# Local and pooled attention feeding a two-layer network: wider column chunks, and pooled rows added straight from their tile

## The chip, the cores and the metric

The kernel runs on one core of a Trainium2 chip. The metric is the device time of one execution in microseconds; a kernel's time is the median of its runs.

## What is computed

For 8 sequences, 8 heads, 576 positions and 64 features a head, two attentions are added: a dense softmax attention over queries, keys and values averaged in groups of 4 (each pooled output row serves 4 positions), and a local one, in which a position sees the 3 positions on either side. The sum, as 4608 rows of 512, goes through a network without biases.

```
out_d  = sm_attn(mean4(q), mean4(k), mean4(v))          # 144 rows a head
out_up = np.repeat(out_d, 4, axis=2)
scores = where(abs(i - j) < 4, scale * q @ k.T, -1e9)   # local, 7 keys a row
x      = out_up + softmax(scores) @ v
h      = x @ w_in                # 4608 x 512 by 512 x 2048
out    = np.maximum(0.01 * h, h) @ w_out                # back to 512
```

## The kernel before

Every matmul of the network is done in three products of a high and a low float32r part: `xh`, `xl` for the rows, `wi` pairs for `w_in`, `woh`, `wol` for `w_out`, `gh`, `gl` for the activations. The rows are the moving columns of TensorE, and they are worked off in **chunks**. `plan()` (L48) lays them out: chunk 0 has 512 columns (the first 512 positions of sequence 0, in two halves of 256), chunk 1 has 256 and chunks 2 to 11 have 384 each. The list `SIZES` gives each chunk its number of blocks: the 576 positions of a sequence are 64 groups of 9, and block j is the j-th position of all 64, 64 columns; 63 blocks belong to sequences 1 to 7.

For each of the 16 tiles f of the inner dimension, `up_proj` (L1038) makes 12 matmuls (4 contraction tiles by 3 products) into a PSUM bank `hp`, and `leaky` (L1067) turns it into `gh` (ScalarE) and `gl` (ScalarE, then VectorE). `down_proj` (L1079) makes 12 matmuls from them into `acc0` to `acc3`. There are three `gh` and three `gl` tiles, so at most three steps stand between up and down. The last two chunks, 10 and 11, are multiplied together in a Strassen scheme (`finale`, L1319), whose combinations T1 to T4 are split by `split_x24` and `split_x31`.

The rows of a chunk come from the local attention, in **segments** of up to three blocks for half the heads (u = 0 or 1): `scores` (L868) multiplies on GpSimd and sums on VectorE, `weigh` does the softmax, `values` (L937) multiplies on GpSimd again and sums on VectorE into an `xloc` tile, of which there are two. `widen` (L984) copies the pooled output `outd` on ScalarE four times along the row into one `up` tile, 576 wide, for each segment. `landing` (L1000) transposes the blocks on TensorE into a `pt` bank (L1007), adds `up` on VectorE (L1013), and splits the sum into high and low part in the chunk's x buffer (L1028, L1030). There are two x buffers, `x0` and `x1`, taken in turn, so chunk i can land once chunk i-2 has been through the up projection.

At the start the weights arrive as float64, in raw tiles (`convert`, L323), and are split: a cast on ScalarE, an integer step (L337) and a subtraction (L350) on VectorE. For f below 9 the raw tiles are the two `prod` tiles, the `up` tile and three staging tiles in `x1`. At the same time sequence 0 goes through a banded form of the local attention, whose pooled output is added at L817.

The order of all instructions is written by a planner in the program (`Order`): tasks ask for slots and engines, the planner holds a modelled clock for each engine and emits the operation that could start first, by rank among equals. So each engine's order is fixed when the program is built, and a change of sizes can move it.

Of the kernel before, what the change touches and what calls it, by code (L numbers as in the profile page):

```python
# [28 lines left out]
SIZES = (3,) + (6,) * 10  # L29
# [48 lines left out]
assert CHUNKS[LAST - 1][1] == EN and LAST % 2  # L78


def pieces(j0, j1):
    n = j1 - j0
    k = -(-n // 3)
    cuts = [j0 + n * i // k for i in range(k + 1)]
    return list(zip(cuts, cuts[1:]))


LANDED = {(i, 0): 2 * sum(len(pieces(a, z)) for _, a, z, _ in c[2]) + (i == 1) for i, c in enumerate(CHUNKS) if i}
LANDED.update({(0, a): NC for a, _ in TOP})
XMAX = [max(c[1] for c in CHUNKS[i:LAST:2]) for i in range(2)]  # L90
# [7 lines left out]
KEPT, LAND = ("x0", "x1", "gh", "gl", "o"), ("xloc", "up", "outd")  # L98
# [111 lines left out]
def attn_moe(ctx: ExitStack, tc, qkt, vm, vr, vmb, vrb, qb, kb, vb, vwb, band, identb, w_in, w_out, ident, edge, out):  # L210
# [76 lines left out]
    heads = [axp.tile([128, DM], I32, name=f"head{i}") for i in range(bufs["head"])]  # L287
# [71 lines left out]
    def outd_tile(b):  # L359
# [3 lines left out]
        t = yield from wait(("read", b), 8 if b < BANDED else 2 * len(PARTS[b]))  # L363
        s.free(t)

    def x_tile(i):
# [500 lines left out]

    def scores(b, j0, j1, u):  # L868
# [19 lines left out]
        for p in range(2):  # L888
            s_q, s_k, q, k, tl = got[p]
            for a, z in pieces(j0, j1):  # L890
                n = z - a
                s_p = yield from slot("prod")
                pr = sb(s_p, [128, 3 * W * D], F32)
                prv = pr[:, :n * W * D].rearrange("p (j t d) -> p j t d", j=n, t=W)
                tp = yield from op("POOL", n * W * D, tl, s_p.t)
                nc.gpsimd.tensor_tensor(  # L896
                    out=prv,
                    in0=q[:, a - j0:z - j0].unsqueeze(2).to_broadcast([128, n, W, D]),
                    in1=view(k, (a - j0) * D, [[D, n], [D, W], [1, D]]),
                    op=ALU.mult)  # L900
                t = yield from op("DVE", n * W * D, tp, s_s.t)
                nc.vector.tensor_reduce(out=s[:, u, p, a - j0:z - j0], in_=prv, axis=AX.X, op=ALU.add)  # L902
                s_p.free(t)
# [33 lines left out]
    def values(i, b, j0, j1, c0, u):  # L937
# [46 lines left out]
    def widen(i, b, j0, j1, u):  # L984
        to = yield from wait(("pooled", b, 2 * u))
        to = max(to, (yield from wait(("pooled", b, 2 * u + 1))))
        tx = yield from wait(("xbuf", i))
        yield from wait(("upturn", ORD[b, j0, u]))
        s_u = yield from slot("up")
        od.signal(("upturn", ORD[b, j0, u] + 1))  # L990
        up = sb(s_u, [128, 2, SD, FAC], F32)
        t = yield from op("ACT", 2 * S, s_u.t, to, times=2)
# [2 lines left out]
        od.signal(("read", b), t)
        ups[b, j0, u] = up
        od.signal(("up", b, j0, u), max(t, tx))
        s_u.free((yield from wait(("upread", b, j0, u), len(pieces(j0, j1)))))

    def landing(i, b, j0, u, a, z, col, s_x, xl_t, t):  # L1000
# [501 lines left out]
```

## Time and profile before

| | |
|---|---|
| median of 3 runs | 911.89 us (911.55 to 912.01) |
| span of the profiled execution, first to last instruction | 910.3 us |
| TensorE busy, matmuls | 897.6 us, 6129 |
| GpSimd, VectorE, ScalarE busy | 625.9, 610.1, 460.9 us |
| DMA | 119.68 MB, 131 GB/s in the mean |

The files give no other time of the profiled execution than its span; the median stands 1.6 us above it. A busy time is the sum of the instructions of an engine; matmuls overlap, so a matmul's own duration is longer than the distance to the next one. PE is TensorE, PEld its weight loads, DVE VectorE, ACT ScalarE, POOL GpSimd. L numbers are lines of the kernel before.

### The profile page before, as it was taken

The numbers are of one execution on the slowest core, as the hardware profiler recorded it, in microseconds if no ns is written. First come the engines' busy times: TensorE is split into PE (matmuls) and PEld (weight loads), VectorE is DVE, ScalarE is ACT, GpSimd is POOL, SyncE is SP. The second block draws the span as 40 slices with busy tenths as digits, with TensorE's granted clock in tenths as the row PEclk, the third lists the DMA queues.
The fourth block names the chain that finished last, engine by engine and source line by source line (L and its number), as shares of the span: only waits on it lengthen the run. The fifth ranks groups of instructions, "written<-read, shape, count | busy, mean of one in ns | idle before, by whom it ended". The sixth has DMA issues, their size and how long they took to land. (4 is left out here: it accounts for less than half of the span.)

```text
span 910.3 us, 16167 instructions
## 1 busy us (share of the span) xinstructions
PE 897.6 (99%) x6129; PEld 870.5 (96%) x6129; DVE 610.1 (67%) x887; ACT 460.9 (51%) x1277; POOL 625.9 (69%) x308
## 2 busy tenths in 40 slices
PE   8999999999999999999999999999999999999998
PEld 4789999999999999999999999999999999999998
DVE  6899889888878977875746863762863755533322
ACT  5788567666455634554324553533413425455332
POOL 4221299989989999967974964982993986787100
PEclk9999999999999999999999999999999999999999
DMA  9786566657646644652522751630431410100001
GB/s 294 257 297 240 174 205 207 199 161 216 199 124 200 210 117 121 207 176 64 153 86 76 213 161 27 176 106 27 122 113 45 122 53 1 36 1 1 1 35 36
DMA packets 61774, 119.68 MB, mean 131 GB/s; under 512 B 7248, under 2 KB 24016, under 8 KB 61696
## 3 DMA queue, kind: packets, MB, share of 16 engines
q1 hardware_dynamic: 61696, 118.65, 42.0%
q8 instruction: 48, 0.79, 0.3%
q14 instruction: 30, 0.25, 0.1%
HBM read 109.18 MB, written 9.44 MB: 130 GB/s over the span
## 5 line engine op out<-in xcount | busy, mean ns | idle before, releaser
L1060 PE MATMUL hp<-x,wi 128*128 128x384 f32 (+1 forms) x2112 | 367.4, 323 | 4.5 <-DVE gl L1074 3.6
L1060 PEld LDWEIGHTS hp<-x,wi 128*128 128x128 f32 x2112 | 338.3, 189 | 8.8 <-DVE gl L1074 4.8
L969 POOL TENSOR_TENSOR prod<-v,s 128x1344 f32<-128x1344 f32 x84 | 261.8, 3124 | 62.2 <-DVE xloc L975 57.6
L896 POOL TENSOR_TENSOR prod<-q,k 128x1344 f32<-128x1344 f32 x84 | 265.9, 3171 | 52.7 <-DVE s L902 27.0
L1098 PE MATMUL acc<-gh,woh 128*128 128x384 f32 (+1 forms) x768 | 252.3, 329 | 0.0
L1098 PE MATMUL acc<-gh,wol 128*128 128x384 f32 (+1 forms) x768 | 247.1, 322 | 0.1
L1098 PE MATMUL acc<-gl,woh 128*128 128x384 f32 (+1 forms) x768 | 246.8, 321 | 0.0
L1071 ACT ACTIVATE gh<-hp 128x384 fp32r<-128x384 f32 (+1 forms) x184 | 85.3, 464 | 223.0 <-PE acc L1098 216.8
L1074 DVE TENSOR_TENSOR gl<-hp,gh 128x384 fp32r<-128x384 f32 (+1 forms) x184 | 95.2, 518 | 133.6 <-ACT hp L1072 130.0
L1098 PEld LDWEIGHTS acc<-gh,woh 128*128 128x128 f32 x768 | 144.8, 189 | 2.5 <-issue 2.0
L1098 PEld LDWEIGHTS acc<-gh,wol 128*128 128x128 f32 x768 | 144.8, 188 | 0.5 <-DVE wol L350 0.5
L1098 PEld LDWEIGHTS acc<-gl,woh 128*128 128x128 f32 x768 | 145.0, 189 | 0.0
L902 DVE TENSOR_REDUCE s<-prod 128x21 f32<-128x1344 f32 x84 | 129.3, 1541 | 13.9 <-POOL prod L896 13.9
L975 DVE TENSOR_REDUCE xloc<-prod 128x192 f32<-128x1344 f32 x80 | 123.4, 1543 | 5.1 <-POOL prod L969 5.1
L1072 ACT ACTIVATE hp<-hp 128x384 f32<-128x384 f32 (+1 forms) x184 | 84.4, 459 | 0.0
L1013 DVE TENSOR_TENSOR pt<-pt,up 128x384 f32<-128x384 f32 x42 | 37.6, 895 | 24.6 <-PE pt L1007 22.4
L994 ACT COPY up<-outd 128x576 f32<-128x576 f32 x84 | 52.1, 672 | 0.0
L425 DVE TENSOR_REDUCE v_d<-vs 128x128 f32<-128x512 f32 (+1 forms) x56 | 37.6, 671 | 5.9 <-DMA vs<-in_vrb_dram 5.0
L1028 ACT CAST x<-pt 128x384 fp32r<-128x384 f32 x38 | 18.4, 484 | 35.7 <-DVE pt L1013 35.7
L783 POOL TENSOR_TENSOR xloc<-xloc,lst 128x280 f32<-128x280 f32 (+1 forms) x8 | 7.3, 919 | 27.0 <-ACT pd L512 12.2
L1170 POOL TENSOR_TENSOR sr<-sr 128x256 f32<-128x256 f32 x32 | 23.8, 758 | 0.9
L1170 POOL TENSOR_TENSOR sr<-wi 128x512 f32<-128x512 f32 x16 | 20.6, 1291 | 3.9 <-DVE pt L1013 3.8
(231 smaller groups left out, 1028.4 us busy)
## 6 DMA issues: line engine op xcount, KB each, us to landing
k<-in_kb_dram SPq DMA_DIRECT2D x84, 288.0 KB, 3.3
v<-in_vb_dram SPq DMA_DIRECT2D x84, 288.0 KB, 2.9
qk<-in_qkt_dram SPq DMA_DIRECT2D x32, 576.0 KB, 4.9
q<-in_qb_dram SPq DMA_DIRECT2D x84, 96.0 KB, 2.0
vs<-in_vmb_dram SPq DMA_DIRECT2D x28, 256.0 KB, 2.8
out_dram<-olot SPq DMA_DIRECT2D x36, 192.0 KB, 2.0
vs<-in_vrb_dram SPq DMA_DIRECT2D x28, 192.0 KB, 3.0
x<-in_w_in_dram SPq DMA_DIRECT2D x9, 511.8 KB, 6.2
```

What stands on the lines that cost most here:

```text
L425: nc.vector.tensor_reduce(out=v_d[:rows, k], in_=vs, axis=AX.X, op=ALU.add)
L896: nc.gpsimd.tensor_tensor(out=prv, in0=q[:, a - j0:z - j0].unsqueeze(2).to_broadcast([128, n, W, D]), in1=view(k, (a - j0) * D, [[D, n], [ ...
L902: nc.vector.tensor_reduce(out=s[:, u, p, a - j0:z - j0], in_=prv, axis=AX.X, op=ALU.add)
L969: nc.gpsimd.tensor_tensor(out=prv, in0=view(v, 0, [[1, nj], [nv, D], [1, W]]), in1=s[:, p, :nj].unsqueeze(2).to_broadcast([128, nj, D, W]) ...
L975: nc.vector.tensor_reduce(out=xl_t[:, :nj, p], in_=prv, axis=AX.X, op=ALU.add)
L994: nc.scalar.copy(out=up[:, pp], in_=outd[b][:, 2 * u + pp].unsqueeze(2).to_broadcast([128, SD, FAC]))
L1060: nc.tensor.matmul(hp[:, :n], w[h][:, ws], x[:, c], start=c + j == 0, stop=c == NC - 1 and j == 2)
L1071: nc.scalar.activation(out=gh[:, :n], in_=hp[:, :n], func=AF.Prelu, alpha=0.01)
L1072: nc.scalar.activation(out=hp[:, :n], in_=hp[:, :n], func=AF.Prelu, alpha=0.01)
L1074: nc.vector.tensor_tensor(out=gl[:, :n], in0=hp[:, :n], in1=gh[:, :n].bitcast(F32), op=ALU.subtract)
L1098: nc.tensor.matmul(acc[:, a:z], w[h][:, es], g[:, :n], start=(a, f, j) == (0, 0, 0), stop=f == NF - 1 and j == 2, skip_group_check=ch == 0)
L1170: (nc.vector if eng == "DVE" else nc.gpsimd).tensor_tensor(out=out, in0=in0, in1=in1, op=alu)
```

## The change

`SIZES` becomes (3, 6, 6, 6, 6, 8, 8, 8, 6, 6): chunk 1 keeps 256 columns, chunks 2 to 5 and 9, 10 have 384, and chunks 6 to 8 have 512. Segments of three blocks stay as they are for `scores`, `weigh` and `values`; where a chunk ends inside one, it lands in two parts, and its `xloc` tile is held until the second. `widen` and the `up` tile are gone: `landing` adds the pooled rows from `outd` in small pieces, one for each run of `RUNS`, in which the pooled row goes on by two. Steps of 256 columns share a `gh` and a `gl` tile by pairs. Both x buffers are 512 wide; the tiles `head` lie in `x1` at first and `edge` in another pool. In the Strassen pair, which is now chunks 9 and 10, T4 lies in the spare columns of one x buffer and in the other.

```diff
-SIZES = (3,) + (6,) * 10
+SIZES = (3, 6, 6, 6, 6, 8, 8, 8, 6, 6)
...
-    parts = {b: [] for b in range(BANDED, B)}
+    parts = {b: [(j, j + MAXSEG, []) for j in range(0, BLK, MAXSEG)] for b in range(BANDED, B)}
...
-            room = min(BLK - j, z - g)
-            m = -(-room // -(-room // MAXSEG))
+            _, j1, lands = parts[b + BANDED][j // MAXSEG]
+            m = min(j1 - j, z - g)
             mine.append((b + BANDED, j, j + m, c0))
-            parts[b + BANDED].append((i + 1, j, j + m, c0))
+            lands.append((i + 1, j, j + m, c0))
...
+def runs(j):
+    at = [(BLK * r + j) // FAC for r in range(FAC)]
+    cuts = [0] + [r for r in range(1, FAC) if at[r] != at[r - 1] + 2] + [FAC]
+    return [(r0, r1, at[r0]) for r0, r1 in zip(cuts, cuts[1:])]
...
-    s = yield from slot(*(("prod", "up") if f < FREE else ("stage2",) if FSPLIT < f < LSPLIT else ()), "stage")
+    s = yield from slot(*(("prod",) if f < FREE else ("stage2",) if FSPLIT < f < LSPLIT else ()), "stage")
...
-        both = sb(s_x, [128, 2, NC, XMAX[i % 2]], F32R)[:, :, :, :CHUNKS[i][1]]
+        whole = sb(s_x, [128, 2, NC, 512], F32R)
+        both = whole[:, :, :, :CHUNKS[i][1]]
+        if i == LAST - 1:
+            fin["spare"] = whole[:, :, :, EN:].rearrange("p h c n -> p (h c) n")
...
-        od.spawn(90 + 10 * b + j0 + 0.5 * u, landing(i, b, j0, u, a, z, c0, s_x, xl_t, t))
+        for k, (i, a, z, col) in enumerate(lands):
+            od.spawn(90 + 10 * b + a + 0.5 * u, landing(i, b, j0, u, a, z, col, s_x, xl_t, t, k == len(lands) - 1))
...
-    def widen(i, b, j0, j1, u):
...
-        for pp in range(2):
-            nc.scalar.copy(out=up[:, pp], in_=outd[b][:, 2 * u + pp].unsqueeze(2).to_broadcast([128, SD, FAC]))
...
-        t = yield from op("DVE", 270 * n, t, tu)
-        nc.vector.tensor_tensor(out=xv, in0=xv, in1=upv, op=ALU.add)
-        od.signal(("upread", b, j0, u), t)
+        adds = [(m, *run) for m in range(n) for run in RUNS[a + m]]
+        t = yield from op("DVE", 128 * n, t, to, times=len(adds))
+        for m, r0, r1, o in adds:
+            part = view(xps, m * 128 + r0, [[NBLK, 2], [FAC, NBLK // FAC], [1, r1 - r0]])
+            nc.vector.tensor_tensor(out=part, in0=part, in1=view(outd[b], 2 * u * SD + o, [[SD, 2], [BLK, NBLK // FAC], [2, r1 - r0]]), op=ALU.add)
...
     def leaky(i, n, s_h, hp, t):
-        s_g, s_l = (yield from slot("gh")), (yield from slot("gl"))
-        gh, gl = sb(s_g, [128, OMAX], F32R), sb(s_l, [128, OMAX], F32R)
+        half = isinstance(i, int) and n == OMAX // 2
+        if half and i % 2:
+            yield from wait(("pair", i // 2))
+            s_g, s_l, gh, gl = pairs.pop(i // 2)
+        else:
+            s_g, s_l = (yield from slot("gh")), (yield from slot("gl"))
+            gh, gl = sb(s_g, [128, OMAX], F32R), sb(s_l, [128, OMAX], F32R)
+            if half:
+                pairs[i // 2] = s_g, s_l, gh[:, n:], gl[:, n:]
...
     def split_x24():
...
+        tx = yield from wait("x1free")
+        t = yield from wait(("T", (0, 1)))
+        hi, lo, src = fin["t4"], fin["spare"][:, :6], raw[0, 1].rearrange("p c (k n) -> p (c k) n", n=512 - EN)
+        t = yield from halve(hi, lo, src, 2 * EN, "DVE", t, tx)
...
     def split_x31():
         yield from wait(("over", LAST - 2))
-        s_x = yield from slot("x1")
+        s_x = yield from slot(f"x{LAST % 2}")
...
+        od.signal("x1free", s_x.t)
```

## Rows read from the trace of the kernel before

**Rows 1.** The page: busy time of each engine, and TensorE's share by 40 slices.

```profile
PE 897.6 (99%) x6129; PEld 870.5 (96%) x6129; DVE 610.1 (67%) x887; ACT 460.9 (51%) x1277; POOL 625.9 (69%) x308
...
PE   8999999999999999999999999999999999999998
```

**Rows 2.** By stretch: length, PE, PEld, DVE, ACT, POOL busy, clock, DMA.

```profile
140.00:160.00 20.00, 19.30 (x168) 18.77 (x168) 19.07 (x27) 14.80 (x47) 19.40 (x7) 1.00 0.62 206
...
850.00:911.00 61.00, 56.61 (x327) 56.29 (x325) 17.11 (x31) 19.39 (x41) 0.00 (x0) 0.98 0.08 27
```

**Rows 3.** Waits of TensorE over the span: total us, times, longest.

```profile
PE hp L1060 <- DVE gl L1074: 3.6, 4, 1.4
...
PE hp L1060 <- DVE wi L350: 0.8, 2, 0.5
```

**Rows 4.** Timeline of TensorE, two early waits: start, us, what, idle before.

```profile
131.49 1.34 PE L1060 MATMUL hp<-x,wi 128*128 128x256 f32 x9 [1.12 <-DVE gl L1074]
...
152.51 3.14 PE L1060 MATMUL hp<-x,wi 128*128 128x256 f32 x24 [0.70 <-DVE gl L1074]
```

**Rows 5.** The chain that ended last, one piece: start, us, what.

```profile
604.18 4.16 PE acc L1098 x24
```

**Rows 6.** Timeline of TensorE, first and last of nine matmuls.

```profile
99.76 0.28 PE L1098 MATMUL acc<-gh,woh 128*128 128x256 f32 x1
...
100.72 0.28 PE L1098 MATMUL acc<-gh,wol 128*128 128x256 f32 x1
```

**Rows 7.** Timeline of TensorE, bfloat16 matmuls of 512 columns.

```profile
9.07 0.60 PE L313 MATMUL acc<-band_sb,idb_sb 128*128 128x512 bf16 x2
...
26.65 0.38 PE L313 MATMUL acc<-band_sb,idb_sb 128*128 128x512 bf16 x1
```

**Rows 8.** Timeline of TensorE around the transposes of one landing.

```profile
767.32 0.49 PE L1007 MATMUL pt<-id_sb,xloc 128*128 128x128 f32 x3
767.57 0.42 PE L1098 MATMUL acc<-gh,woh 128*128 128x384 f32 x1
767.83 0.34 PE L1098 MATMUL acc<-gl,woh 128*128 128x384 f32 x1
768.00 0.34 PE L1098 MATMUL acc<-gh,wol 128*128 128x384 f32 x1
```

**Rows 9.** The page's costliest groups: busy us, mean ns | idle before.

```profile
L969 POOL TENSOR_TENSOR prod<-v,s 128x1344 f32<-128x1344 f32 x84 | 261.8, 3124 | 62.2 <-DVE xloc L975 57.6
L896 POOL TENSOR_TENSOR prod<-q,k 128x1344 f32<-128x1344 f32 x84 | 265.9, 3171 | 52.7 <-DVE s L902 27.0
...
L994 ACT COPY up<-outd 128x576 f32<-128x576 f32 x84 | 52.1, 672 | 0.0
```

**Rows 10.** Groups of VectorE by shape, same columns.

```profile
L1013 DVE TENSOR_TENSOR pt<-pt,up 128x384 f32<-128x384 f32 x42 | 37.6, 895 | 24.6 <-PE pt L1007 22.4 <-ACT olot L1140 1.1 <-ACT up L994 0.6
...
L817 DVE TENSOR_TENSOR pt<-pt,outd 128x320 f32<-128x320 f32 x4 | 2.0, 494 | 0.3 <-PE pt L806 0.2
...
L817 DVE TENSOR_TENSOR acc<-acc,outd 128x256 f32<-128x256 f32 x4 | 1.7, 430 | 0.4 <-PE acc L806 0.4
```

**Rows 11.** Groups of VectorE by shape: the conversions through `up`.

```profile
L337 DVE SCALAR_TENSOR_TENSOR up<-up,head 128x512 int32<-128x512 int32 x3 | 2.1, 690 | 0.2
...
L350 DVE TENSOR_TENSOR wol<-up,woh 128x512 fp32r<-128x512 f32 x3 | 2.1, 688 | 0.0
```

**Rows 12.** Timelines of ScalarE and GpSimd where the Strassen pair begins.

```profile
779.67 0.84 ACT L1174 CAST t<-r 128x768 fp32r<-128x768 f32 x1
780.40 1.76 ACT L1174 CAST x<-r 128x768 fp32r<-128x768 f32 x2
...
782.24 2.43 POOL L1170 TENSOR_TENSOR x<-r,x 128x768 fp32r<-128x768 f32 x1 [4.49 <-ACT x L1174]
```

**Rows 13.** Timeline of GpSimd as the x buffer of chunk 7 opens.

```profile
490.16 6.16 POOL L969 TENSOR_TENSOR prod<-v,s 128x1344 f32<-128x1344 f32 x2 [11.80 <-DVE xloc L975]
```

**Rows 14.** Timeline of VectorE: first `gl` of chunks 6 and 7.

```profile
498.00 0.55 DVE L1074 TENSOR_TENSOR gl<-hp,gh 128x384 fp32r<-128x384 f32 x1
...
570.66 0.58 DVE L1074 TENSOR_TENSOR gl<-hp,gh 128x384 fp32r<-128x384 f32 x1
```

More of the change, by code (lines that the diff above doesn't have):

```diff
@@ L77 @@
 EN = CHUNKS[LAST][1]
[L78 to L88, printed above, removed]
+assert CHUNKS[LAST - 1][1] == EN
+LANDED = {(i, 0): 2 * len(c[2]) + (i == 1) for i, c in enumerate(CHUNKS) if i}
 LANDED.update({(0, a): NC for a, _ in TOP})
-XMAX = [max(c[1] for c in CHUNKS[i:LAST:2]) for i in range(2)]
 OMAX = max(c[1] for c in CHUNKS[1:])
@@ L97, with __init__, __getitem__ @@
 SCARCE, HURRY = ("pt",), 1000
-KEPT, LAND = ("x0", "x1", "gh", "gl", "o"), ("xloc", "up", "outd")
+KEPT, LAND = ("x0", "x1", "gh", "gl", "o"), ("xloc", "outd")
+class Cut:
+    def __init__(self, ap, n):
+        self.ap, self.n = ap, n
+    def __getitem__(self, at):
+        return self.ap[:, at[1] * self.n:(at[1] + 1) * self.n]
+def runs(j):
+    at = [(BLK * r + j) // FAC for r in range(FAC)]
+    cuts = [0] + [r for r in range(1, FAC) if at[r] != at[r - 1] + 2] + [FAC]
+    return [(r0, r1, at[r0]) for r0, r1 in zip(cuts, cuts[1:])]
+RUNS = [runs(j) for j in range(BLK)]
 def view(ap, offset, dims):
@@ L285, in attn_moe @@
     w_out_v = w_out.rearrange("(f p) e -> f p e", p=128)
-    heads = [axp.tile([128, DM], I32, name=f"head{i}") for i in range(bufs["head"])]
+    stage = [wk.tile([128, bufs["stage"] + 1, HALFS * DM], U16, name="x1", tag="x1", bufs=bufs["x1"])]
+    heads = [stage[0][:, bufs["stage"], i * 2 * DM:(i + 1) * 2 * DM].bitcast(I32) for i in range(bufs["head"])]
     for h in heads:
@@ L362, in outd_tile @@
         od.signal(("outd", b), s.t)
-        t = yield from wait(("read", b), 8 if b < BANDED else 2 * len(PARTS[b]))
+        t = yield from wait(("read", b), 8 if b < BANDED else 2 * sum(len(p[2]) for p in PARTS[b]))
         s.free(t)
@@ L863, in attn_moe @@
     for b in PARTS:
-        for _, a, z, _ in PARTS[b]:
+        for a, z, _ in PARTS[b]:
             VOFF[b, a] = n
@@ L889, in scores @@
             s_q, s_k, q, k, tl = got[p]
[L890 to L903, printed above, removed]
+            s_p = yield from slot("prod")
+            pr = sb(s_p, [128, 3 * W * D], F32)
+            prv = pr[:, :nj * W * D].rearrange("p (j t d) -> p j t d", j=nj, t=W)
+            tp = yield from op("POOL", nj * W * D, tl, s_p.t)
+            nc.gpsimd.tensor_tensor(
+                out=prv,
+                in0=q[:, :nj].unsqueeze(2).to_broadcast([128, nj, W, D]),
+                in1=view(k, 0, [[D, nj], [D, W], [1, D]]),
+                op=ALU.mult)
+            t = yield from op("DVE", nj * W * D, tp, s_s.t)
+            nc.vector.tensor_reduce(out=s[:, u, p, :nj], in_=prv, axis=AX.X, op=ALU.add)
+            s_p.free(t)
             s_q.free(tp)
@@ L979, in values, with landing @@
         od.signal("values", t)
-        od.spawn(90 + 10 * b + j0 + 0.5 * u, landing(i, b, j0, u, a, z, c0, s_x, xl_t, t))
-    ups = {}
-    def widen(i, b, j0, j1, u):
[L985 to L992, printed above, removed]
-        for pp in range(2):
-            nc.scalar.copy(out=up[:, pp], in_=outd[b][:, 2 * u + pp].unsqueeze(2).to_broadcast([128, SD, FAC]))
[L995 to L1000, printed above, removed]
+        for k, (i, a, z, col) in enumerate(lands):
+            od.spawn(90 + 10 * b + a + 0.5 * u, landing(i, b, j0, u, a, z, col, s_x, xl_t, t, k == len(lands) - 1))
+    def landing(i, b, j0, u, a, z, col, s_x, xl_t, t, last):
         n = z - a
-        tu = yield from wait(("up", b, j0, u))
+        to = max((yield from wait(("pooled", b, 2 * u))), (yield from wait(("pooled", b, 2 * u + 1))))
+        to = max(to, (yield from wait(("xbuf", i))))
         s_b = yield from slot("pt")
@@ L1101, in down_proj @@
                     od.spawn(-5, store(ch, e, s_a, acc, t))
-            s_g.free(t)
-            s_l.free(t)
+            if not (isinstance(i, int) and n == OMAX // 2 and i % 2 == 0):
+                s_g.free(t)
+                s_l.free(t)
             if i == ("g", NF - 2):
@@ L1115, in outbuf @@
         yield from wait(("done", LAST - 1))
-        s_x = yield from slot("x0")
+        s_x = yield from slot(f"x{(LAST - 1) % 2}")
         first.append(sb(s_x, [128, NE, 512], F32))
@@ L1163, in make_room @@
         od.signal(("xbuf", LAST), t)
-        t = yield from wait("landed", len(ORD))
+        t = yield from wait("landed", sum(LANDED[i, 0] for i in range(1, LAST + 1)) - 1)
         at.__exit__(None, None, None)
@@ L1207, in split_x24 @@
         s_t = yield from slot("t24")
-        pair = unit(2, "t24", [128, 2, 2, 2, EN], F32R)
-        for k, (j, h) in enumerate((("T2", 0), ("T4", 1))):
-            t = yield from wait(("T", (0, h)))
-            T[j] = [pair[:, k, m] for m in range(2)]
-            t = yield from halve(T[j][1], T[j][0], raw[0, h], 2 * EN, "DVE", t, tc2)
-            od.signal(j, t)
+        pair = unit(2, "t24", [128, 2, 2, EN], F32R)
+        T["T2"] = [pair[:, m] for m in range(2)]
+        t = yield from wait(("T", (0, 0)))
+        t = yield from halve(T["T2"][1], T["T2"][0], raw[0, 0], 2 * EN, "DVE", t, tc2)
+        od.signal("T2", t)
+        tx = yield from wait("x1free")
+        t = yield from wait(("T", (0, 1)))
+        hi, lo, src = fin["t4"], fin["spare"][:, :6], raw[0, 1].rearrange("p c (k n) -> p (c k) n", n=512 - EN)
+        t = yield from halve(hi, lo, src, 2 * EN, "DVE", t, tx)
+        T["T4"] = [Cut(x, EN // (512 - EN)) for x in (lo, hi)]
+        od.signal("T4", t)
         od.signal("x24", t)
```

46 lines of the change are left out of this document (25 added, 21 removed).

## The prediction

> **What bounds the kernel now.** I read the share of each engine first: TensorE is busy 897.6 of 910.3 us, and its line over the span shows only the first slice and the last one short of a 9 [rows 1]. No other engine comes near that over the whole, but in single stretches one does, so the table by stretch was next: from 140 to 160 us VectorE is busy 19.07 of 20 us and GpSimd 19.40, the only part where they run as full as TensorE; in the last 61 us nothing but TensorE works hard [rows 2]. A busy TensorE may still be waiting between two matmuls, so I looked at what it waited for: 3.6 us for the low half `gl` from VectorE and 0.8 us for a weight split on VectorE (`wi`) [rows 3]. Where those waits stand is seen in the timeline: early, at 131 and 152 us for instance [rows 4]. After that the matmuls of the two projections follow each other without a hole, so the time is the sum of the pitches of TensorE's instructions, and the question is what one matmul costs as a function of its columns.
>
> The chain that ended last gives the pitch at 384 columns: 24 down-projection matmuls in 4.16 us, 173.3 ns each [rows 5]. The timeline at 256 columns: eight steps from 99.76 to 100.72 us, 120.0 ns each [rows 6]. The difference, 53.3 ns for 128 columns, is 0.417 ns a column; that is the 2.4 GHz level, and the granted clock in the table by stretch is 1.00 [rows 2]. What is left is the same for both sizes: 120.0 - 106.7 = 13.3 ns, and 173.3 - 160.0 = 13.3 ns. So a matmul pays 13.3 ns that no column accounts for, and fewer, wider matmuls save it. No float32 matmul of 512 columns is in this trace; two bfloat16 ones are, back to back: 0.60 us for two and 0.38 for one, so 0.22 us apart [rows 7], at the recorded resolution what 512 x 0.4167 + 13.3 = 226.7 ns asks for.
>
> **The change part by part.**
>
> *One chunk fewer.* Columns stay at 4608 in all. Before, ten chunks have 384 columns; after, six have 384 and three have 512. Chunks 6 to 8 hold 1536 columns, which were four chunks. A chunk costs 16 f-tiles x (12 up + 12 down) = 384 matmuls. Before: 4 x 384 = 1536 matmuls x 173.3 ns = 266.2 us. After: 3 x 384 = 1152 x 226.7 ns = 261.2 us. The gain is 384 x 13.3 ns = 5.1 us, all on the path. The Strassen pair at the end keeps its two chunks of 384.
>
> *Landings split at chunk borders.* The chunks end at blocks 35 and 43, inside segments 33-36 and 42-45. So 21 segments give 23 landings a head half, 46 in place of 42. The 126 transposes stay, but each group of transposes breaks the weight prefetch: the matmul behind it starts 0.25 us later, and the next one 0.26 instead of 0.17 [rows 8]. The 0.09 us extra is paid per group, so four more groups cost 0.4 us; the bounds are 0 and four whole groups of one or two transposes, 4 x 0.25 = 1.0 us. I take 0.4.
>
> *Pooled output without the widened copy.* ScalarE loses 84 copies of 0.672 us, 52.1 us [rows 9]. It was 51% busy, so by itself this is worth nothing on the path. On VectorE 42 adds of 0.895 us become small adds: of nine blocks three need one add (128 elements), six need two (96 and 32), 15 per nine, 210 in all. The nearest row is the add of a pooled row into PSUM in sequence 0: 0.430 us for 256 elements, 0.494 for 320 [rows 10], which is 1.0 ns an element and 0.174 us fixed. That gives 0.302, 0.270 and 0.206 us, so 3 x 0.302 + 6 x 0.476 = 3.76 us per nine blocks, 14 times: 52.7 us in place of 37.6, 15 us more. From below: with no fixed cost 16.1 us, 21 us less. From above: the old add's slope, (0.895 - 0.174)/384 = 1.88 ns an element, gives 66.8 us, 29 us more. I take the nearest row, 15 us, because it has the same operands. VectorE is busy 67%, so what covers it is its idle time; only from 140 to 160 us, with 0.9 us idle [rows 2], could it show. The adds lengthen each landing by 0.36 us and two or three landings fall there: between 0 and 1.0 us lost, and I take 0, since the same change loosens the wait in the next part.
>
> *Shared tiles for 256-column steps.* The first 48 steps (chunks 0 and 1) have 256 columns. `gh` and `gl` now hold 512 columns and two such steps share one, so six steps can stand between up and down projection, not three. TensorE's waits on VectorE, 4.4 us in all [rows 3], lie almost all in these steps; a longer backlog of down-projection work can cover some: at most the two of rows 4 and the weight waits, 2.6 us. The opposite sign: the `up` tile is gone as a place for raw weights. Three of 32 conversions used it [rows 11]; each keeps VectorE 0.69 + 0.69 = 1.4 us, and if each of the three came late by that, TensorE would lose 4.1 us. I take 0 for the two together and keep -2.6 and +4.1.
>
> *The end.* The T4 split now waits for the x buffer, with T3 and T1. Before, ScalarE's casts at 779.67 and 780.40 and a GpSimd subtraction to 784.7 us made the pair [rows 12] while TensorE ran on, and P4 comes behind 18 matmuls, 3.1 us. One cast (0.84 us) and one VectorE subtraction are added to that chain; two or three down steps of 12 x 0.227 = 2.7 us stand before it. Cover 5.4 + 3.1 us against some 5 us: nothing.
>
> Sum against the profiled execution's span: 910.3 - 5.1 + 0.4 = 905.6 us. The median of the runs, 911.9, is 1.6 us above that span, for what lies around it, and I keep the 1.6: **907.2 us**.
>
> **The rivals.**
>
> *Weights late at the start.* For it: the weight waits are there already [rows 3] and a staging tile is gone. Against: only three of 32 used it [rows 11]. It needs 2 to 4.1 us to matter: 909.2 to 911.3 us.
>
> *The backlog pays.* The paired tiles take the early waits away: 907.2 - 2.6 = 904.6 us. For it: the waits on `gl` are the largest; against: the order of each engine is fixed by the planner, which may put the room elsewhere.
>
> *The step isn't constant.* If a matmul above 384 columns grew in proportion, 173.3 x 512/384 = 231.1 ns, then 1152 x 231.1 = 266.2 us, as before, and only the 0.4 us is left: 912.3 us. For it: only two float32 sizes are in the trace. Against: from 256 to 384 it did not grow so (120.0 against 115.6). The same mechanism in a weaker form, where most of the 13.3 ns is gone again at 512 columns, ends between 907.2 and 912.3 us. The Trainium skill speaks for it ("TensorE: Matmul & The Clock Gate", "Wait — 56ns, not 53.3ns?"): it gives about 2.5 ns as the fixed cost of a warm matmul, start to start; an estimate by it would be 384 x 2.5 ns = 1.0 us of gain and 911.3 us. By that rule the trace does not agree: the rows of this kernel have 13.3 ns at both sizes [rows 5, 6].
>
> *Landings late at a 512 chunk: slower.* Chunk 7 needs blocks 35 to 42. With the x buffer open, three fresh segments must be made, because the tiles of segment 33-36 stay held for block 35. A segment is four score and four value multiplies on GpSimd, 4 x 3.17 + 4 x 3.12 = 25.2 us [rows 9], some 26 with the small steps; three make 79 us. In before the same buffer opened at about 490 us, where GpSimd restarts after waiting 11.8 us for `xloc` [rows 13]; so it would be done at 569, and landed at about 572. Chunk 6 starts at 498 us by its first `gl`, and the next one 72.7 us later [rows 14]; with 20.5 us more for the wide matmuls (87.0 - 66.6) the need comes at 591 us. That is 19 us in hand, and more where scores are made ahead. From 19 us of delay on, each microsecond costs one. To be slower than before by more than a measurement can tell it would take some 26 us. At that point 913.8 us.
>
> **How the numbers follow.** Main case 0.69, with 905.6 to 908.6 as its own range (adds and groups at their bounds). Backlog pays 0.12, weights late 0.10, step not constant or small 0.05, landings late 0.04. A measurement of this kernel tells about 0.2%, 1.8 us, from no change, so faster means below 910.1. Faster: 0.69 + 0.12 + 0.06 of the late weights = 0.87. Same: the other 0.04 of them + 0.05 = 0.09. Slower: 0.04. The range runs from the backlog case, 904.5, to 909.9, which leaves out the two rivals without a gain and most of the late weights, some 0.16.
>
> **What would show it.** TensorE: 384 matmuls fewer, and 24 down-projection matmuls of 512 columns in 5.44 us. ScalarE without the copy, some 50 us less busy. VectorE's small adds near 0.2 to 0.3 us, 15 us more in all. GpSimd's two big rows unchanged. No wait of TensorE at the start of chunks 6 to 8. The prediction is wrong if 512 columns take clearly over 227 ns, if the first 150 us move by more than 3 us, or if a hole stands before a 512 chunk.

## The result, and the profile after

The changed kernel takes **919.3 us** (median of four runs, 918.8 to 919.9) where the kernel before, on the same chip, takes 911.7 us (911.5 to 912.0): ratio 1.0085, interval 1.0073 to 1.0097. It is slower by 7.6 us; 907.2 us was forecast, with a range of 904.5 to 909.9. The profiled execution's span went from 910.3 to 917.8 us.

The page of the kernel after, its engines and its costliest groups [rows 1, 9]:

```profile
PE 900.3 (98%) x5745; PEld 821.7 (90%) x5745; DVE 629.9 (69%) x1043; ACT 410.2 (45%) x1161; POOL 626.2 (68%) x308
...
L904 POOL TENSOR_TENSOR prod<-q,k 128x1344 f32<-128x1344 f32 x84 | 264.8, 3155 | 68.8 <-DVE s L910 45.8
L977 POOL TENSOR_TENSOR prod<-v,s 128x1344 f32<-128x1344 f32 x84 | 261.2, 3115 | 42.9 <-DVE xloc L983 40.8
...
L1007 DVE TENSOR_TENSOR pt<-pt,outd 128x64 f32<-128x64 f32 (+3 forms) x210 | 53.9, 259 | 39.6 <-PE pt L999 33.1
```

TensorE has 384 matmuls fewer, ScalarE 51 us less work, VectorE 20 us more, GpSimd the same. (L1007 is now the small add, L999 the transposes, L1054 and L1102 the two projections, L1075 to L1078 `leaky`, L344 the integer step of a weight split.) The chain that ended last, two pieces in a 512-column chunk (start, us, what), as in [rows 5]:

```profile
574.03 5.44 PE hp L1054 x24
579.47 5.44 PE acc L1102 x24
```

24 matmuls of 512 columns in 5.44 us are 226.7 ns each, to the digit the pitch forecast. So the saving is there, 384 x 13.3 ns = 5.1 us, and the loss is larger. The small adds by shape (us in total, mean ns), as in [rows 10]:

```profile
L1007 DVE TENSOR_TENSOR pt<-pt,outd 128x96 f32<-128x96 f32 x56 | 15.7, 280 | 1.9
...
L1007 DVE TENSOR_TENSOR pt<-pt,outd 128x64 f32<-128x64 f32 x56 | 14.0, 250 | 17.9 <-PE pt L999 16.4
L1007 DVE TENSOR_TENSOR pt<-pt,outd 128x128 f32<-128x128 f32 x42 | 12.4, 299 | 8.2 <-PE pt L999 6.8 <-ACT st_d L692 0.5
L1007 DVE TENSOR_TENSOR pt<-pt,outd 128x32 f32<-128x32 f32 x56 | 12.0, 218 | 11.6 <-PE pt L999 9.9 <-ACT hp L1076 0.3
```

They cost 53.9 us in all; 52.7 was forecast. The table by stretch of the kernel after (columns as in [rows 2]) shows where TensorE is not full:

```profile
30.00:70.00 40.00, 36.92 (x412) 33.91 (x411) 36.21 (x79) 30.53 (x84) 6.34 (x5) 1.00 0.77 252
70.00:80.00 10.00, 7.90 (x59) 7.49 (x58) 9.62 (x15) 6.76 (x19) 4.64 (x2) 0.92 0.95 349
80.00:90.00 10.00, 10.00 (x79) 10.00 (x79) 7.77 (x16) 7.94 (x21) 0.00 (x0) 0.91 0.60 180
...
140.00:150.00 10.00, 10.00 (x87) 10.00 (x86) 9.52 (x19) 5.57 (x21) 8.86 (x4) 1.00 0.63 203
150.00:160.00 10.00, 8.51 (x56) 6.92 (x55) 9.82 (x16) 4.94 (x15) 9.91 (x6) 0.83 0.77 248
...
760.00:830.00 70.00, 70.00 (x364) 64.88 (x364) 21.85 (x37) 30.59 (x60) 46.18 (x42) 1.00 0.04 15
```

Two places stand out, 70 to 80 and 150 to 160 us. In before TensorE was busier there, at a granted clock of 1.00; in after the clock falls behind the holes in both.

```profile
70.00:80.00 10.00, 9.85 (x83) 9.65 (x82) 9.69 (x19) 8.99 (x27) 3.59 (x1) 1.00 0.96 366
...
150.00:160.00 10.00, 9.30 (x84) 8.77 (x83) 9.69 (x14) 7.17 (x24) 9.53 (x4) 1.00 0.79 274
```

What TensorE waited for in the whole span, as in [rows 3]:

```profile
PE hp L1054 <- DVE gl L1078: 4.0, 10, 1.4
PE hp L1054 <- DVE wi L357: 2.8, 3, 2.0
...
PE acc L1102 <- DVE wol L357: 0.9, 1, 0.9
PE pt L999 <- DVE xloc L983: 0.8, 1, 0.8
```

The wait for a weight grew from 0.8 to 2.8 us. That is the hole at 75 us; the timeline of GpSimd, VectorE and TensorE around it:

```profile
72.32 3.52 POOL L904 TENSOR_TENSOR prod<-q,k 128x1344 f32<-128x1344 f32 x1 [1.19 <-DVE wol L357]
...
73.09 3.30 DVE L344 SCALAR_TENSOR_TENSOR x<-x 128x512 int32<-128x512 int32 x1
76.31 0.68 DVE L357 TENSOR_TENSOR wi<-x,wi 128x512 fp32r<-128x512 f32 x1
...
74.68 0.40 PE L1054 MATMUL hp<-x,wi 128*128 128x256 f32 x2
```

The integer step takes 3.30 us, where its median over 19 is 0.69: it ends 0.55 us after GpSimd's multiply does, and the weight that TensorE wants comes behind it. In before the same multiply came at 75.82, and the integer step that met it (78.61 us, 1.36 us long) ended 0.56 us after it as well, but met only its last 0.8 us.

**Counting every hole.** The waits listed are only the larger ones. So I took the time from the start of each group of matmuls to the start of the next, and subtracted the group's own pitches (columns / 2400 us + 13.3 ns; + 26.7 ns for the 128 and 144 column transposes, as such rows show back to back). What is left, in us by stretch, holds waits and slow clock alike. The rows e1 to e17 are the experiments further down:

| kernel | 0-30 | 30-110 | 110-165 | 165-235 | 235-760 | 760-830 | sum |
|---|---|---|---|---|---|---|---|
| before | 6.1 | 3.5 | 3.8 | 1.5 | -0.2 | 1.1 | 16.0 |
| after | 5.8 | 7.7 | 6.0 | 3.5 | 4.8 | 0.3 | 28.1 |
| e1 one raw tile fewer | 6.8 | 7.2 | 7.2 | 1.6 | -1.1 | 1.2 | 23.1 |
| e2 small adds alone | 5.9 | 3.8 | 6.2 | 3.4 | 3.7 | 3.4 | 26.5 |
| e3 old chunk sizes | 6.7 | 6.5 | 7.8 | 3.9 | 3.6 | 3.2 | 31.8 |
| e4 adds priced as measured | 7.0 | 7.2 | 7.6 | 4.7 | 0.6 | 0.3 | 27.5 |
| e5 raw tile back | 5.9 | 7.0 | 9.1 | 2.2 | 4.7 | 0.3 | 29.4 |
| e6 the two together | 5.8 | 5.5 | 9.2 | 2.7 | 1.0 | 0.3 | 24.6 |
| e13 early order of before | 6.9 | 4.6 | 4.8 | 5.1 | 3.1 | 0.3 | 25.1 |
| e14 and priced | 6.0 | 4.6 | 4.6 | 5.3 | -0.3 | 0.3 | 20.6 |
| e16 and copies on ScalarE | 6.9 | 4.5 | 5.9 | 2.0 | 1.2 | 0.3 | 21.0 |
| e17 and shared tiles | 6.9 | 5.5 | 8.6 | 2.0 | 1.0 | 0.3 | 24.5 |

After has 12.1 us more holes than before; less the 5.1 us of matmuls that is 7.0, and the span grew by 7.5. So the loss is in two parts: 8.4 us from 30 to 235 us, and 5.0 us spread thinly from 235 to 760. Only at 760 to 830 did holes close.

The second part has a face. The chain of waits of the kernel after, at 520 us (start, us, what):

```profile
520.04 0.49 ACT hp L1076
520.53 0.12 ACT st_d L692
520.65 0.20 issue
520.85 0.31 DVE pt L1007
...
521.18 0.30 DVE pt L1007
...
521.51 0.23 DVE pt L1007
...
521.77 0.27 DVE pt L1007
...
522.06 0.24 DVE pt L1007
522.30 0.60 DVE gl L1078
522.91 0.04 issue
522.95 3.02 PE hp L1054 x12
```

ScalarE is done with `hp` at 520.53, which `gl` needs; when `gl` is through, the bank comes free that TensorE wants for its next step. But `gl` stands behind five small adds of one landing: 522.30 - 520.85 = 1.45 us. In before one add, 0.895 us in the mean, did this work. The planner has all five at 0.80 us (128 elements a block by its rate, and its fixed part of an instruction five times), little more than half of what they take, and so puts them in front of a `gl` that has no such time to give. TensorE still had matmuls to do for most of that time; the hole here is 0.3 us.

From 235 to 760 us seven holes are longer than 0.25 us, 3.2 us together. In four of them, at 314, 522, 551 and 744 us, `gl` is behind small adds. In the other three, at 361, 390 and 690 us, it is behind a sum into `xloc` (L983), as in this piece of the chain:

```profile
688.18 1.54 DVE xloc L983
689.72 0.61 DVE gl L1078
690.38 2.37 PE hp L1054 x9
```

The matmul at 690.38 is the first of chunk 8. A planner that thinks VectorE free too early can misplace these sums too; whether the low price does it is tested below.

### The profile page after: what moved, and what is told of

The parts are those of the page before. It is cut to its first block, busy times and chain, and to the rows that moved or that the text cites. A ratio compares the mean times of both kernels' runs of the same rounds, so it can differ in the third digit from the quotient of the medians.

```text
span 917.8 us, 15458 instructions
## 1 busy us (share of the span) xinstructions
PE 900.3 (98%) x5745; PEld 821.7 (90%) x5745; DVE 629.9 (69%) x1043; ACT 410.2 (45%) x1161; POOL 626.2 (68%) x308
## 4 chain that ended last, share of the span: by engine, by line
PE 86%; DVE 8%; DMA 2%; ACT 2%; issue 1%; SPq 0%; ACTq 0%; DVEq 0%
PE acc L1102 36%; PE hp L1054 33%; PE pt L1359 5%; PE hp L1359 2%; PE hp L1102 2%; PE pt L1102 2%; DVE pt L1007 2%; DMA qk<-in_qkt_dram 2%; PE pt L999 1%; DVE xloc L983 1%; DVE gl L1078 1%; PE pt L649 1%; DMA x<-in_w_out_dram 1%; DVE x L344 1%; PE pt L500 1%
## 5 line engine op out<-in xcount | busy, mean ns | idle before, releaser
L1054 PE MATMUL hp<-x,wi 128*128 128x384 f32 (+2 forms) x1920 | 364.6, 340 | 7.1 <-DVE gl L1078 4.0
L1054 PEld LDWEIGHTS hp<-x,wi 128*128 128x128 f32 x1920 | 312.9, 190 | 38.1 <-DVE gl L1078 9.6
L1102 PE MATMUL acc<-gh,woh 128*128 128x384 f32 (+2 forms) x704 | 241.7, 343 | 0.0
L1102 PE MATMUL acc<-gh,wol 128*128 128x384 f32 (+2 forms) x704 | 236.7, 336 | 1.0 <-DVE wol L357 0.9
L1102 PE MATMUL acc<-gl,woh 128*128 128x384 f32 (+2 forms) x704 | 236.3, 336 | 0.0
L1075 ACT ACTIVATE gh<-hp 128x384 fp32r<-128x384 f32 (+2 forms) x168 | 82.4, 491 | 203.7 <-PE acc L1102 194.7
L1078 DVE TENSOR_TENSOR gl<-hp,gh 128x384 fp32r<-128x384 f32 (+2 forms) x168 | 92.3, 553 | 106.3 <-ACT hp L1076 105.0
L1102 PEld LDWEIGHTS acc<-gh,wol 128*128 128x128 f32 x704 | 133.0, 189 | 9.2 <-DVE wol L357 1.4
L1102 PEld LDWEIGHTS acc<-gh,woh 128*128 128x128 f32 x704 | 133.1, 189 | 8.4 <-issue 1.0
L1102 PEld LDWEIGHTS acc<-gl,woh 128*128 128x128 f32 x704 | 133.3, 189 | 7.1
L983 DVE TENSOR_REDUCE xloc<-prod 128x192 f32<-128x1344 f32 x80 | 123.2, 1544 | 8.5 <-POOL prod L977 8.4
L1076 ACT ACTIVATE hp<-hp 128x384 f32<-128x384 f32 (+2 forms) x168 | 82.0, 488 | 0.0
L1007 DVE TENSOR_TENSOR pt<-pt,outd 128x64 f32<-128x64 f32 (+3 forms) x210 | 53.9, 259 | 39.6 <-PE pt L999 33.1
L1024 DVE TENSOR_TENSOR x<-pt,x 128x384 fp32r<-128x384 f32 (+2 forms) x42 | 21.5, 514 | 2.2 <-ACT x L1022 0.9
```

The costliest lines, as they stand in the source:

```text
L983: nc.vector.tensor_reduce(out=xl_t[:, :nj, p], in_=prv, axis=AX.X, op=ALU.add)
L1007: nc.vector.tensor_tensor(out=part, in0=part, in1=view(outd[b], 2 * u * SD + o, [[SD, 2], [BLK, NBLK // FAC], [2, r1 - r0]]), op=ALU.add)
L1054: nc.tensor.matmul(hp[:, :n], w[h][:, ws], x[:, c], start=c + j == 0, stop=c == NC - 1 and j == 2)
L1075: nc.scalar.activation(out=gh[:, :n], in_=hp[:, :n], func=AF.Prelu, alpha=0.01)
L1076: nc.scalar.activation(out=hp[:, :n], in_=hp[:, :n], func=AF.Prelu, alpha=0.01)
L1078: nc.vector.tensor_tensor(out=gl[:, :n], in0=hp[:, :n], in1=gh[:, :n].bitcast(F32), op=ALU.subtract)
```

## Experiments

In all of them "the price" is only the planner's number for an instruction: a change of it alters the order of the same instructions and nothing else. HOP, a planner constant of 0.2 us, is of that kind too. The expectations weigh three causes against each other: the small adds (their time on VectorE, or the place that a low price gives them); the tiles (the raw tile that is gone, so that weights come late, and the shared ones); and the planner's order as such, which any edit deals anew. A is the theory of the tiles, B that of the adds, and C that of the order.

**One part at a time.** e1 takes from before the use of the `up` tile for raw weights and pooled products; e2 takes `widen` out of before and adds from `outd` as after does; e3 gives after the old sizes, and with them the shared tiles go too, as `leaky` shares only steps of half the widest chunk (192 columns there, and no step has those); e4 gives after's adds the price that they have on the chip.

```diff
# e1 (before)
-    s = yield from slot(*(("prod", "up") if f < FREE else ...
+    s = yield from slot(*(("prod",) if f < FREE else ...
...
-    ... (yield from slot(*(("v", "up") if pool else ("pd",))))
+    ... (yield from slot("v" if pool else "pd"))
# e2 (before)
-        t = yield from op("DVE", 270 * n, t, tu)
-        nc.vector.tensor_tensor(out=xv, in0=xv, in1=upv, op=ALU.add)
+        t = yield from op("DVE", 128 * n, t, to, times=len(adds))
+        for m, r0, r1, o in adds:
...
-                    od.spawn(90 + r, widen(i, b, j0, j1, u))
# e3 (after)
-SIZES = (3, 6, 6, 6, 6, 8, 8, 8, 6, 6)
+SIZES = (3,) + (6,) * 10
# e4 (after)
-        t = yield from op("DVE", 128 * n, t, to, times=len(adds))
+        t = yield from op("DVE", 128 * n + 125 * len(adds), t, to, times=len(adds))
```

> The kernel before, with only the raw weight place `up` taken from the conversions (and from the pooled rows of sequence 0). Theory A (the loss of the first 160 us is the missing raw tile: weights late, so the first local scores late, so chunk 1 late): 915 to 918 us, with the first hole of TensorE at about 75 us and the third GpSimd score multiply at about 112 us instead of 105.7. Theory B (the loss is the small adds, VectorE's and the planner's price for them): 911 to 913 us.

> The kernel before, with only the widened copy replaced by the small adds from `outd`; the `up` tile stays for the raw weights, the chunks stay at 384. Theory A: 911 to 913 us, as the adds lie on VectorE's idle time. Theory B: 915 to 919 us, the waits of TensorE for `gl` two to three times those of before (3.6 us), spread over the whole span.

> The changed kernel with the old list of chunk sizes (eleven chunks after the first, none of 512 columns), all else as changed. If a matmul pays 13.3 ns that no column accounts for, 384 more of them cost 5.1 us less 0.4 us of landing groups: 923.5 to 924.5 us. Rival (the 512-column chunks bring waits of their own, so that their gain is lost): 917 to 921 us.

> The changed kernel; only the planner's price of a landing's adds is raised from 0.80 us to 1.45 us for three blocks (measured start to start 1.45 us), so the instructions are the same and only their order moves. Theory B: the small holes in front of the up projection after 200 us, some 4.7 us more than before, shrink to half or less: 915 to 917 us. Theory A: 918.5 to 920 us.

Before took 911.1 us in these runs. e1: 919.1 us, 1.0084 (1.0067 to 1.0101). e2: 925.0, 1.0155 (1.0137 to 1.0173). e3: 929.6, 1.0207 (1.0190 to 1.0224). e4: 917.1, 1.0068 (1.0052 to 1.0085). e1, e2 and e3 came out above both of their ranges, e4 at the upper end of B's. By their times, each of two parts alone costs as much as the whole change or more. The chunk sizes pay: of the 929.6 - 919.3 = 10.3 us of e3, 5.1 are matmuls and 2.9 the holes at 760 to 830 us (3.2 against 0.3; no row of the table with 512-column chunks has more than 0.3 there, none without them less than 1.1). The rest can be the shared tiles or the order. e1 shows the same held integer steps as after, two in 4.24 us:

```profile
71.30 4.24 DVE L337 SCALAR_TENSOR_TENSOR x<-x,head 128x512 int32<-128x512 int32 x2
```

and e2 shows that TensorE waits for `gl` twice as long as in [rows 3] (line numbers of e2):

```profile
PE hp L1071 <- DVE gl L1085: 7.5, 10, 1.5
```

e4 empties the stretch from 235 to 760 us (4.8 to 0.6), but the holes from 110 to 235 us grow by 1.6 + 1.2 us, so the time moves by only 2.2 us.

**The raw tile, the multiplies, and the order by itself.** e5 gives after a tile of its own for raw weights, and holds the pool in which it lies until those weights are split; e6 is e5 with e4's price; e8 lets no score multiply begin before the last weights are nearly split; e7 is before with HOP at 0.21.

```diff
# e5, e6 (after)
-    s = yield from slot(*(("prod",) if f < FREE else ...
+    s = yield from slot(*(("prod", "raw") if f < 7 else ("prod",) if f < FREE else ...
# e8 (after), in scores
+        yield from wait("converted", 2 * NF - 6)
# e7 (before)
-HOP = 0.2
+HOP = 0.21
```

> The changed kernel with a sixth place for raw weights again, for f below 7, in the pool that sequence 0 leaves later; the adds and the chunk sizes as changed. Theory A (the missing raw tile costs what it cost alone, some 7 us, by the VectorE step held at 73 us behind a GpSimd multiply and by later weights): 911.5 to 914 us, no hole at 75 us. Rival (the early loss comes with the adds anyway): 917 to 920 us.

> The same with the planner's price of the adds at 1.45 us for three blocks. If the two losses add up and both are mended: 908.5 to 912 us, faster than before or equal. If the adds cost VectorE time that no order can hide in the stretch from 140 to 220 us: 913 to 917 us.

> The kernel before; only the planner's allowance for a hop from engine to engine goes from 0.20 to 0.21 us. The same instructions and tiles, in another order. Theory C (before is a lucky order, and any shift of the planner costs as much as the parts of the change did): 915 us or more. Theories A and B (tiles and adds, not the order as such): 910 to 913 us.

> The changed kernel; the local scores start only when 26 of the 32 weight conversions are emitted, so the two `prod` tiles serve raw weights in that time instead of holding two products that VectorE sums only at 110 us, and no GpSimd multiply stands beside the conversions. Theory A: the hole at 75 us (2.1 us) is gone and the weights come earlier, 914.5 to 917 us. If the local attention's start is what counts, not the weights, it is late by as much again: 920 us or more.

Before: 911.3. e5: 921.5, 1.0106 (1.0089 to 1.0123); the tile alone mends nothing, and a hole of 1.9 us before a weight stands at 80 us. e6: 916.9, 1.0056 (1.0041 to 1.0071): again the price by itself takes the holes from 235 to 760 us away, 4.7 to 1.0 us, and here the time goes with them, by 4.6 us. e8: 930.6, 1.0208 (1.0191 to 1.0226): TensorE's holes are 38.2 us, so holding the multiplies off early is no cure. e7: 923.8, 1.0136 (1.0121 to 1.0151). e5 came out above both of its ranges, e6 and e8 in the second of theirs, e7 in theory C's. e7 has the instructions of before, one planner constant a twentieth larger, and is 12.5 us slower. So before's order is a lucky one, and a comparison of two kernels compares two draws as well. That holds for e1, e2, e3 and e5 too: their times differ from those they are held against by no more than draws do, 8 to 14 us, and what they show lies in the rows and holes of their traces.

**Is it only the draw?** before and after at HOP 0.19 and 0.22.

```diff
-HOP = 0.2
+HOP = 0.19   # e9 (before), e11 (after)
+HOP = 0.22   # e10 (before), e12 (after)
```

> The kernel before with the planner's hop at 0.19 us in place of 0.20: same instructions, another order. Theory C (the order of before is an outlier that holds TensorE without a hole through the first 220 us): 918 to 926 us, with holes and a fallen clock between 60 and 220 us. Theories A and B: 910 to 913 us.

> The same with the hop at 0.22 us. Theory C: 918 to 926 us. Theories A and B: 910 to 913 us.

> The changed kernel with the hop at 0.19 us. Theory C: it scatters as before does, but some 5 us lower, as its matmuls save 5.1 us in any order: 913 to 921 us. Theories A and B: it stays where it is, 918 to 921 us.

> The same with the hop at 0.22 us. Theory C: 913 to 921 us, and the mean of the two and of the changed kernel itself some 5 us below the mean of the shaken kernels before. Theories A and B: 918 to 921 us.

| HOP | before | after | difference |
|---|---|---|---|
| 0.19 | 924.1 | 926.2 | 2.0 |
| 0.20 | 911.7 | 919.3 | 7.6 |
| 0.22 | 914.8 | 920.7 | 5.9 |

The row of 0.20 is the result above; beside the other four kernels before took 910.6 us. The ratios to that are 1.0147 (1.0117 to 1.0176), 1.0050 (1.0027 to 1.0073), 1.0169 (1.0140 to 1.0199) and 1.0109 (1.0080 to 1.0138), for e9 to e12. e9 came out in theory C's range and e12 in both ranges, e10 and e11 in neither. The draw is worth up to 14 us, but after is the slower at each value, at 0.19 by 2.0 us with intervals that overlap: three draws do not show the gain that was forecast. From 235 to 760 us the holes of after are 3.3 and 3.6 us in e11 and e12, those of before -0.8 and 1.7 in e9 and e10: that part goes with the adds and their price, not with the draw (e1, without the adds, has -1.1; e2 and e3, with them, 3.7 and 3.6).

**The early order held fixed.** e13 is after with a tile that takes the old `up` tile's two uses (in the early pool, held as in e5), without the shared `gh` and `gl` tiles, so that in the traces VectorE's first 190 instructions and ScalarE's first 205 stand as in before. That is up to before's first widened copy, which starts at 103 us, and to 107 us on VectorE, not to 135 us as was expected. e14 is e13 with the measured price, e15 with the price of the one old add.

```diff
# e13 (after)
-    s = yield from slot(*(("prod",) if f < FREE else ...
+    s = yield from slot(*(("prod", "up") if f < 7 else ("prod",) if f < FREE else ...
...
-    ... (yield from slot("v" if pool else "pd"))
+    ... (yield from slot(*(("v", "up") if pool else ("pd",))))
...
-        half = isinstance(i, int) and n == OMAX // 2
+        half = False
# e14 (e13)
+        t = yield from op("DVE", 128 * n + 125 * len(adds), t, to, times=len(adds))
# e15 (e13)
+        t = yield from op("DVE", 270 * n, t, to)
```

> The changed kernel with the early places of before, so that VectorE's and ScalarE's order is that of before until the first widened copy would come, at about 135 us; chunks of 512, small adds, price 0.80 us as changed. Theory C2 (the early loss is the order): holes from 30 to 165 us as before, some 7 to 8 us, no fallen clock at 75 us: 910 to 913 us. Theory D (the changed parts cost there in any order): 917 us or more.

> The same with the adds priced at 1.45 us for three blocks. Theory C2 and B together: the 4 us of holes after 235 us go as well: 905.5 to 909 us, faster than both. Theory D: 914 us or more.

> The same with the price of the old single add, 0.92 us for three blocks, so that the order of VectorE after 135 us is nearer to that of before, too. If a price near the old one is what keeps the order: 906 to 910 us. If the price must be the true one to keep the small holes away: between the two others, 909 to 912 us.

Before: 911.3. e13: 917.1, 1.0064 (1.0049 to 1.0079). e14: 912.7, 1.0016 (1.0007 to 1.0026). e15: 916.8, 1.0055 (1.0037 to 1.0074). e13 came out in theory D's range, e14 and e15 in none of theirs; a price of 0.92 us (e15) gains only 0.3 us. In the stretch where the order was held, 30 to 110 us, e13 has 4.6 us of holes, after 7.7 and before 3.5; from 165 to 235 us it has more than both, 5.1 us. e13 and e14 have the same instructions and the same mean clock, 1.00; they differ in the price alone, by 4.4 us of time, and the holes from 235 to 760 us by 3.1 + 0.3 = 3.4. The chain of waits from 235 to 760 us, shares by line, of after, e13 and e14 in turn:

```profile
by line: PE hp L1054 44.8%; PE acc L1102 41.1%; DVE pt L1007 2.2%; PE pt L999 1.9%; issue 1.2%; PE pt L649 1.2%; DMA qk<-in_qkt_dram 1.1%; DVE gl L1078 1.1%; DVE xloc L983 1.0%; PE pt L712 0.8%; PE pt L668 0.7%; PE pt L671 0.6%; ACT hp L107
```

```profile
by line: PE hp L1054 45.7%; PE acc L1102 42.6%; PE pt L999 1.8%; DVE pt L1007 1.7%; PE pt L649 1.3%; DVE xloc L983 1.1%; PE pt L668 1.0%; DVE gl L1078 0.9%; PE pt L712 0.8%; PE pt L671 0.8%; issue 0.7%; ACT hp L1076 0.4%; ACT gh L1075 0.3%;
```

```profile
by line: PE hp L1054 47.0%; PE acc L1102 45.7%; PE pt L999 2.1%; PE pt L649 1.3%; PE pt L668 1.0%; PE pt L712 0.9%; PE pt L671 0.8%; PE pt L713 0.3%; DVE pt L1007 0.3%; issue 0.2%; PE pt L600 0.1%; DVE s L910 0.1%; DVE x L1024 0.1%; PE pt L
```

The small adds stand on the chain with 2.2% of 525 us, 1.7% and 0.3%; `gl` (L1078) with 1.1%, 0.9% and none that is shown. That settles the second part of the loss: three pairs that differ in the price alone (after and e4, e5 and e6, e13 and e14) lose these holes with it. The adds' time on VectorE is covered there (e14 has as many); the order that their low price made was not.

**What is left early.** e14 still loses 5.3 us at 165 to 235, where VectorE is fuller than in before (33.01 of the 35 us from 200 on, 30.35 in before) while ScalarE has nearly half its time free. e16 is e14 with the two output copies of chunk 0 that VectorE makes (1.27 us for both in after) put on ScalarE. e17 is e16 with the shared tiles of after.

```diff
# e16 (e14)
-        if ch in (0, LAST - 2, LAST) and e % 2:
+        if ch in (LAST - 2, LAST) and e % 2:
# e17 (e16)
-        half = False
+        half = isinstance(i, int) and n == OMAX // 2
```

> As e14 (early places of before, adds priced at 1.45 us), and chunk 0's two output copies that VectorE made at about 149 us (0.68 us each) go to ScalarE. If VectorE's load is what opens the holes at 149 to 152 us (2.7 us in e14): 909.5 to 911.5 us, holes from 140 to 160 us down by 1 us or more. If only the order counts: 912 to 914 us.

> As e16, with the shared gh and gl tiles for the steps of 256 columns as in the change, which moves the early order away from that of before. If the longer backlog pays by itself: 907 to 909.5 us. If the order of before is what keeps TensorE fed early: 913 to 918 us.

Before: 910.9. e16: 910.1 us, 0.9996 (0.9987 to 1.0005), no difference that can be told; the time is as expected for VectorE's load, but not the place of the gain. e17: 915.6, 1.0057 (1.0043 to 1.0071). The tables by stretch of e14, e16 and e17 in turn:

```profile
140.00:160.00 20.00, 17.94 (x149) 16.80 (x148) 18.58 (x34) 9.85 (x33) 19.07 (x8) 1.00 0.58 193
200.00:235.00 35.00, 32.35 (x213) 31.07 (x212) 33.01 (x56) 19.66 (x67) 32.89 (x14) 1.00 0.68 205
```

```profile
140.00:160.00 20.00, 18.19 (x138) 17.05 (x138) 17.91 (x34) 11.52 (x39) 19.92 (x8) 0.91 0.68 227
200.00:235.00 35.00, 35.00 (x247) 33.92 (x246) 31.73 (x55) 19.97 (x67) 33.50 (x16) 1.00 0.62 195
```

```profile
140.00:160.00 20.00, 15.75 (x120) 14.46 (x119) 18.78 (x33) 12.26 (x43) 19.23 (x10) 0.86 0.74 255
```

With VectorE at 31.73 of 35 us where it had 33.01, TensorE is full from 200 to 235 us, and the holes at 165 to 235 go from 5.3 to 2.0. From 140 to 160 us, where the two copies were and where the gain was expected, TensorE is busy hardly more (18.19 against 17.94), at a clock of 0.91. (The profiled execution is the longest of its eleven, 911.9 us, so the sum of its holes does not show the gain of the median.) e17, with the shared tiles and the order that comes with them, is 5.5 us slower, in the range for the order: TensorE is busy 15.75 us of the 20 where it was 18.19. e16 is the best of the kernels with the wide chunks and the small adds, 9 us below after, and no better than before: its holes, 21.0 against 16.0 us, take what the matmuls save.

## Why the prediction was wrong, step by step

**One chunk fewer: right.** 5.44 us for 24 matmuls at 512 columns, 384 fewer, 5.1 us. The rule of the Trainium skill that was weighed against it ("TensorE: Matmul & The Clock Gate", "Wait — 56ns, not 53.3ns?", about 2.5 ns a matmul) does not hold here: 226.7 ns less 512 / 2400 us leaves 13.3 ns. The sizes closed holes at 760 to 830 us as well, 3.2 to 0.3 us from e3 to after, which the forecast did not count.

**Landings split, the end: nothing against them.** From 760 to 830 us the holes are 0.3 us in place of 1.1. Before chunks 6 and 7 there is no hole above 0.15 us. Before chunk 8 there is one of 0.45 us, which was named as a sign of being wrong; but TensorE waits there for `gl`, not for rows that land, so the rival of late landings did not come about. What the four more groups of transposes cost, 0.4 us in the sum, was not measured by itself.

**The adds: the size right, "I take 0" wrong.** The 15 us were 16.3 (53.9 - 37.6); two of the six blocks of two adds split as 64 and 64, not 96 and 32, which by the forecast's line costs the same. What failed is the step from "VectorE is busy 67%, so what covers it is its idle time" to nothing. VectorE's order is fixed; a `gl` behind an add waits for it, however idle the engine is a microsecond later. Adds of 1.45 us were priced at 0.80, and in the order that this made `gl` stood behind adds or sums at places all the way to 760 us. That cost 4 to 5 us (4.8 us of holes in after; 4.4 us of time from e13 to e14). The bounds for the adds had been 0 to 1.0 us, for 140 to 160 us alone.

**Shared tiles and the missing tile: "I take 0 for the two together" wrong.** From 30 to 235 us the kernel after lost 8.4 us. The forecast's bounds were -2.6 and +4.1, and its own sign of being wrong, 3 us in the first 150, came. The shared tiles were to give up to 2.6 us; with them e17 is 5.5 us slower than e16, so the rival "the backlog pays" is not borne out, though the order moved as well. The rival "weights late at the start" came nearest: a weight wait of 2.0 us is there. But its price (three conversions of 1.4 us) was not its mechanism. The conversions do end later (the last integer step starts at 105.5 us, 100.3 in before), but TensorE's wait comes from one of them alone, which ran into a GpSimd multiply that the new order had put 3.5 us earlier and stood for 2.6 us. And the tile given back alone (e5) does not mend it. With before's places and order up to about 105 us (e13), 3.1 of the 4.2 us lost from 30 to 110 us come back; which of the parts does it is not told apart.

**The premise under all of it.** Every price above was laid on before's order, as though that stood still, and as though its early stretch were an ordinary one. The forecast named the planner once, in a rival. The order after is another draw, and e7 and e9 show that draws alone differ by 12 to 14 us, more than any term of the sum. The range of the main case was added up wrongly as well: with the groups and the adds at their bounds it is 906.8 to 908.8 us, not 905.6 to 908.6; the measured time is outside both.

What stays open: the step from 1.0016 to 0.9996 between e14 and e16, 1.8 us, looks like VectorE's load at 140 to 235 us, but the order changed with it. How the 8.4 us divide between load, shared tiles and order is not settled; the 3.6 us that e16 still has over before from 30 to 235 us neither.

## What to carry to other kernels

Where a program plans its own order, give the planner the measured duration of each instruction that an edit brings, before anything else is concluded: the same adds cost 4.4 us (e13 to e14) by a price little more than half of the real one. Work put on a partly idle engine is free only where nothing that the bottleneck waits for is queued behind it, so look for the short producer (`gl` here) behind the new work and not at the busy share. And shake the plan by a constant that means nothing before trusting a difference of one per cent between two plans.

## What the runs showed of the hardware

VectorE's integer step was held until GpSimd's multiply was through: 3.30 us in place of 0.69, its end 0.55 us behind the multiply's (0.56 in before). The Trainium skill ("SBUF — State Buffer", "Terms") says that the two engines share a port pair that one instruction holds for its whole length, and that the loser blocks fully; the trace agrees for these steps.

In after, TensorE's clock fell behind holes: with the 2.1 us hole at 75 us the mean granted clock is 0.92 from 70 to 80 us and 0.91 from 80 to 90, and 0.83 from 150 to 160 us around holes of 0.8, 0.7 and 1.0 us; a part of each of these stretches ran at the 1.2 GHz level, the rest at 2.4. Not every such hole does it: in e14 TensorE is busy only 17.94 of the 20 us from 140 to 160, and the granted clock is 1.00 there. By after's rows the low level took (0.08 + 0.09 + 0.17) x 10 = 3.4 us of full speed, an estimate, which is part of the 8.4 us of holes. How much of it reaches the end is not shown, and it seems little: the four runs of after have mean clocks of 0.996, 1.000, 0.994 and 0.998 and spans of 917.8, 917.2, 918.2 and 917.0 us, so the one at 1.000 is at most 1.0 us shorter than any other.
